# Re-laying a matrix product's input by DMA: 128-token blocks, repeated pooled rows and paired tokens in a fused attention and mixing kernel

## The chip, the cores and the metric

The kernel runs on one core of one Trainium2 chip. The time is the device time of that core, in microseconds (us). Every quoted time is a median of several executions, with the range behind it. Each execution is labelled fast or slow: with one core, a run is called slow when it is over 1.5% above the fastest run of the same kernel. The trace also gives the mean granted TensorE clock, as a share of full speed.

The engines are named as in the profile: PE (matmuls), PEld (weight loads, which overlap PE), DVE (VectorE), ACT (ScalarE), POOL (GpSimd) and SP (SyncE, which here does nothing but issue DMAs). "SPq" lines are DMA issues in SP's instruction stream. An issue is only the handing over of a transfer; the bytes move later, on 16 DMA engines.

## The reference, cut to what matters

There are 8 batches, 8 heads, 576 tokens and 64 numbers per head, so the model width is 512.

```python
def _attn_ref(q, k, v):                      # q, k, v: [8, 8, 576, 64]
    q_d, k_d, v_d = means over groups of 4 tokens        # 144 pooled tokens
    out_d = softmax_attention(q_d, k_d, v_d)
    out_up = np.repeat(out_d, 4, axis=2)                 # back to 576 tokens
    mask = np.abs(pos[:, None] - pos[None, :]) < 4
    out_local = masked softmax attention of q, k, v
    return out_up + out_local

def _moe_ref(x, w_theta, w_tok_r, w_tok_i, w_ch):        # x: [8, 576, 512]
    theta = x @ w_theta
    zr, zi = x * cos(theta), x * sin(theta)
    y = w_tok_r @ zr + w_tok_i @ zi                      # over the 576 tokens
    u = x + y
    return u + relu(u @ w_ch)
```

## The kernel before

The program emits three generators in an interleaved order: `attention(b+1)`, `modulate(b)` and `mix(b-1)`. One round of the three is called a batch period here. The names of the PSUM tiles name the steps:

- `attention`: `pstr` transposes q and k and pools them in the same matmul, `psvd` pools v, `psSd` and `psnd` are pooled scores and pooled output, `psS` and `psloc` are banded scores and local output, and `psup` repeats the pooled rows.
- `modulate`: `xTps` transposes x, and `psth` is theta.
- `mix`: `psu` is the token mix, `psr` and `psx` make the result.

The local attention works on five chunks of 120 tokens (the last has 96), and these chunks are kept through `modulate` and the token mix. So the token mix has 5 chunks x 2 (cosine and sine) = 10 steps of contraction, each with 120 of 128 rows in use.

```python
QS = [0, 120, 240, 360, 480]; QC = [120, 120, 120, 120, 96]      # query chunks
...
def load_qk(b):                                  # on SP, 256-byte rows
    for nm, src in (("q", q), ("k", k)):
        ...                                      # six DMAs each
        nc.sync.dma_start(out=t[:, c, :, :],
            in_=src[b, :, TR*c:TR*c+TR, :].rearrange("h p d -> p h d"))
...
    for h in range(H):                           # pooled output, K = 72 twice
        for kk in range(2):
            nc.tensor.matmul(out=pv[0:QD, h // 4, h % 4, :],       # psnd
                lhsT=pd[:, kk, h, QD*g:QD*g+QD], rhs=vd[:, kk, h, 0:65], ...)
...
    for c in range(NCH):                         # repeat pooled rows on PE, add on DVE
        nc.tensor.matmul(out=up[0:qn, :], lhsT=RT[g][:, QS[c]:QS[c]+qn],   # psup
                         rhs=xd[:, g, :], ...)
        ... psloc matmuls, rl = 1 / sum, tmp = psloc * rl ...
        nc.vector.tensor_tensor(out=x[0:cnt], in0=tmp[0:cnt], in1=up[0:cnt], op=ALU.add)
...
    # token mix: 4 x 5 x 2 x 2 = 80 matmuls per batch
    nc.tensor.matmul(out=pss[hf][:, 0:288],                        # psu
        lhsT=z[0:QC[c], c, ri, P*dc:P*dc+P],
        rhs=WT[0:QC[c], ri, c, 288*hf:288*hf+288], ...)
```

The softmax here doesn't subtract the row's maximum and nothing guards it: scores larger than these inputs give would overflow.

Of the kernel before, what the change touches and what calls it, by code (L numbers as in the profile page):

```python
# [13 lines left out]
P = 128  # L14
# [16 lines left out]
NCH = 5  # L31
TR = 96
NTR = S // TR
TP = TR // 4
TW = TR + TP

OS = [0, 128, 256, 384, 512]
OC = [128, 128, 128, 128, 64]
# [3 lines left out]
def kernel(  # L42
# [16 lines left out]
    xpool = ctx.enter_context(tc.tile_pool(name="xpool", bufs=1))  # L59
# [14 lines left out]
    def load_qk(b):  # L74
        ts = []
        for nm, src in (("q", q), ("k", k)):
            t = work.tile([TR, NTR, H, D], FP32, tag=f"{nm}32", bufs=1, name=f"{nm}32_{b}")
            for i in range(2):
                for c in range(3 * i, 3 * i + 3):
                    nc.sync.dma_start(  # L80
                        out=t[:, c, :, :],
                        in_=src[b, :, TR * c:TR * c + TR, :].rearrange("h p d -> p h d"),
                    )
            ts.append(t)
        staged[b] = ts

    def load_v(b):
        t = work.tile([P, NCH, H, D], FP32, tag="v32", bufs=1, name=f"v32_{b}")
        for c in range(NCH):
            nc.sync.dma_start(  # L90
                out=t[0:KW[c], c, :, :],
                in_=v[b, :, KS[c]:KS[c] + KW[c], :].rearrange("h p d -> p h d"),
            )
        staged[b].append(t)

    def cast(b, engines):

        q32, k32, v32 = staged.pop(b)
        q_tm = work.tile([TR, NTR, H, D], BF16, tag="q_tm", bufs=1, name=f"q_tm{b}")
        k_tm = work.tile([TR, NTR, H, D], BF16, tag="k_tm", bufs=1, name=f"k_tm{b}")  # L100
        v_w = work.tile([P, NCH, H, 66], BF16, tag="v_w", name=f"v_w{b}")
        inputs[b] = (q_tm, k_tm, v_w)
        nc.vector.memset(v_w[:, :, :, 64:65], 1.0)
        for eng, dst, src in ((engines[0], q_tm, q32), (engines[1], k_tm, k32)):
            for i in range(2):
                eng(out=dst[:, 3 * i:3 * i + 3], in_=src[:, 3 * i:3 * i + 3])  # L106
                yield
        engines[2](out=v_w[:, 0:2, :, 0:D], in_=v32[:, 0:2])
        yield
        engines[2](out=v_w[:, 2:4, :, 0:D], in_=v32[:, 2:4])  # L110
        engines[2](out=v_w[0:KW[4], 4, :, 0:D], in_=v32[0:KW[4], 4])
        yield

    load_qk(0)
    load_v(0)

# [5 lines left out]

    ip = const.tile([TR, TW], BF16, name="ip")
    nc.vector.memset(ip[:, TR:TW], 0.25)
    nc.gpsimd.affine_select(out=ip[:, TR:TW], in_=ip[:, TR:TW], compare_op=ALU.is_ge, fill=0.0,
                            base=0, pattern=[[-4, TP]], channel_multiplier=1)
    nc.gpsimd.affine_select(out=ip[:, TR:TW], in_=ip[:, TR:TW], compare_op=ALU.is_ge, fill=0.0,
                            base=3, pattern=[[4, TP]], channel_multiplier=-1)
    nc.vector.tensor_copy(out=ip[:, 0:TR], in_=ident[0:TR, 0:TR])  # L129

    pihc = const.tile([P, 1], FP32, name="pihc")
    nc.vector.memset(pihc, PIH)

    first = cast(0, (nc.vector.tensor_copy, nc.gpsimd.tensor_copy, nc.scalar.copy))
    for _ in range(4):
        next(first)
# [6 lines left out]
    for lo, hi, sh, w in ((0, 120, 0, QD), (4, 124, 59, 144)):  # L143
# [13 lines left out]
    def pool_mat(g, c):  # L157
        o = 0 if c == 0 else 59 - (KS[c] - 288 * g) // 4
        return PU[min(c, 1)][0:KW[c], o:o + QD]


    ru = const.tile([QD, 288 + S], BF16, name="ru")
    nc.vector.memset(ru, 1.0)
    nc.gpsimd.affine_select(out=ru, in_=ru, compare_op=ALU.is_ge, fill=0.0,
                            base=-288, pattern=[[1, 288 + S]], channel_multiplier=-4)
    nc.gpsimd.affine_select(out=ru, in_=ru, compare_op=ALU.is_ge, fill=0.0,
                            base=291, pattern=[[-1, 288 + S]], channel_multiplier=4)
    RT = [ru[:, 288 - 288 * g:288 - 288 * g + S] for g in range(2)]


    w_tm = []
    for ri, w_dram in enumerate((moe_w_tok_r, moe_w_tok_i)):
        t = moep.tile([P, 5, S], BF16, tag="uT", name=f"wtm{ri}")
        nc.gpsimd.dma_start(out=t[:, 0:4, :], in_=w_dram[0:512, :].rearrange("(c p) e -> p c e", p=P))
        nc.gpsimd.dma_start(out=t[0:64, 4, :], in_=w_dram[512:576, :])
        w_tm.append(t)
    wch = wpool.tile([P, 4, DM], BF16, name="wch")
    nc.gpsimd.dma_start(out=wch, in_=moe_w_ch.rearrange("(c p) e -> p c e", p=P))
    WT = wpool.tile([P, 2, NCH, S], BF16, name="WT")

    def build_WT():
        for ri in range(2):
            for c in range(NCH):
                ps = w1(f"wps{ri}{c}", BF16)
                for ct in range(5):
                    rows = OC[ct]
                    nc.tensor.transpose(  # L187
                        out=ps[0:QC[c], ct * P:ct * P + rows],
                        in_=w_tm[ri][0:rows, ct, QS[c]:QS[c] + QC[c]],
                        identity=ident[0:rows, 0:rows],  # L190
                    )
                nc.vector.tensor_copy(out=WT[0:QC[c], ri, c, :], in_=ps[0:QC[c], 0:S])
                yield
# [4 lines left out]
    def attention(b):  # L198
        q_tm, k_tm, v_w = inputs.pop(b)
        if b + 1 < B:  # L200
            load_qk(b + 1)
            load_v(b + 1)
        ahead = cast(b + 1, (nc.gpsimd.tensor_copy,) * 3) if b + 1 < B else iter(())
        qT = work.tile([P, 4, S], BF16, tag="qT", name=f"qT{b}")
        kT = work.tile([P, 4, S], BF16, tag="kT", name=f"kT{b}")
        qdT = work.tile([P, 4, SD], BF16, tag="qdT", name=f"qdT{b}")
        kdT = work.tile([P, 4, SD], BF16, tag="kdT", name=f"kdT{b}")
        for n, (tm, To, Tdo) in enumerate(((q_tm, qT, qdT), (k_tm, kT, kdT))):
            for hh in range(4):
                ps = w2(f"pstr{n}{hh}_{b}")  # L210
                for c in range(NTR):
                    nc.tensor.matmul(  # L212
                        out=ps[:, c // 3, (c % 3) * TW:(c % 3) * TW + TW],
                        lhsT=tm[:, c, 2 * hh:2 * hh + 2, :],
                        rhs=ip,
                        start=True, stop=True,
                    )
                pv = ps[:, :, 0:3 * TW].rearrange("p k (c w) -> p k c w", w=TW)
                nc.scalar.copy(  # L219
                    out=To[:, hh, :].rearrange("p (k c w) -> p k c w", k=2, c=3),  # L220
                    in_=pv[:, :, :, 0:TR],
                )
                nc.vector.tensor_copy(
                    out=Tdo[:, hh, :].rearrange("p (k c w) -> p k c w", k=2, c=3),
                    in_=pv[:, :, :, TR:TW],
                )
                yield

        vd = work.tile([QD, 2, H, 66], BF16, tag="vd", name=f"vd{b}")
        nc.vector.memset(vd[:, :, :, 64:65], 1.0)  # L230
        for g, cs in ((0, (0, 1, 2)), (1, (2, 3, 4))):
            ps = w1(f"psvd{g}_{b}")
            for c in cs:
                nc.tensor.matmul(
                    out=ps[0:QD, :],
# [4 lines left out]
            nc.scalar.copy(out=vd[:, g, :, 0:D], in_=ps[0:QD, :].rearrange("p (h d) -> p h d", d=D))  # L240
# [3 lines left out]
        pd = work.tile([QD, 2, H, SD], BF16, tag="pd", name=f"pd{b}")  # L244

        def pooled_scores(dst, kk, hh):
            for par in range(2):
                nc.tensor.matmul(
                    out=dst(par),
                    lhsT=kdT[64 * par:64 * par + 64, hh, QD * kk:QD * kk + QD],  # L250
# [4 lines left out]
        for kk in range(2):  # L255
            ps = w2(f"psSd{kk}_{b}")
            for hh in range(3):
                pooled_scores(lambda par: ps[0:QD, par, SD * hh:SD * hh + SD], kk, hh)
            nc.scalar.activation(  # L259
                out=pd[:, kk, 0:6, :].rearrange("p (j e) w -> p e j w", e=2),  # L260
                in_=ps[0:QD, :, 0:3 * SD].rearrange("p e (j w) -> p e j w", w=SD),
                func=AF.Exp, scale=SCL,
            )
            yield
        ps = w2(f"psSd2_{b}")
        for kk in range(2):
            pooled_scores(lambda par: ps[0:QD, par, SD * kk:SD * kk + SD], kk, 3)
        nc.scalar.activation(
            out=pd[:, :, 6:8, :].rearrange("p k e w -> p e k w"),
            in_=ps[0:QD, :, 0:2 * SD].rearrange("p e (k w) -> p e k w", w=SD),  # L270
            func=AF.Exp, scale=SCL,
        )
        yield
# [3 lines left out]
        for c in range(NCH):  # L277
            kw, qn = KW[c], QN[c]
            ps = w2(f"psS{c}_{b}")
            for hh in range(4):  # L280
                for par in range(2):
# [6 lines left out]
            pm = work.tile([P, 8, P], BF16, tag="pm", bufs=6, name=f"pm{c}_{b}")  # L288
            nc.scalar.activation(  # L289
                out=pm[0:kw, :, 0:qn],  # L290
# [3 lines left out]
            off = KS[c] - QS[c] + 3  # L294
            nc.gpsimd.affine_select(out=pm[0:kw, :, 0:qn], in_=pm[0:kw, :, 0:qn],  # L295
                                    compare_op=ALU.is_ge, fill=0.0,
                                    base=off, pattern=[[0, 8], [-1, qn]], channel_multiplier=1)
            nc.gpsimd.affine_select(out=pm[0:kw, :, 0:qn], in_=pm[0:kw, :, 0:qn],  # L298
                                    compare_op=ALU.is_ge, fill=0.0,
# [156 lines left out]
    def drain(gen):  # L456
        for _ in gen:
            pass
# [55 lines left out]
```

## Time and profile before

| what | before |
|---|---|
| time | 359.72 us, median of 3 (359.23 to 360.01); 359.87 with a fourth run, which the ratio below counts |
| span in the trace, granted clock | 358.8 us, 0.955 |
| first `psth` (end of the prologue) | 63.4 us |
| distances between the first `psth` of successive batches | 33.4, 38.2, 37.7, 37.8, 36.1, 36.1, 35.4 us |
| last first-`psth` to the end | 40.7 us |

These lines are from the page of the kernel before: busy time by engine, and the span in 40 slices of 9 us (a digit is the busy share of a slice in tenths; the last row is what the DMA engines moved).

```profile
PE 296.6 (83%) x2834; PEld 201.8 (56%) x2834; DVE 193.5 (54%) x435; ACT 192.1 (54%) x283; POOL 156.2 (44%) x153
...
PE   0025689948799989999899989998999899979995
...
GB/s 151 200 187 198 181 154 156 193 178 14 48 200 27 5 180 173 195 53 175 179 195 79 117 218 174 118 145 153 0 3 62 74 0 3 81 53 2 117 16 132
```

PE is the busiest engine and, after the prologue, stays near 9 tenths. The first six slices are low on PE while the DMA row is at its highest: the prologue is fed by DMA.

These are two windows of 4 us from the windows view of one period of the kernel before. The columns are the window, its length, then busy us and instruction count of PE, PEld, DVE, ACT and POOL, then the clock, the DMA share and the GB/s.

```profile
203.00:207.00 4.00, 3.81 (x39) 2.12 (x36) 4.00 (x9) 0.71 (x2) 1.70 (x2) 1.00 0.62 171
...
219.00:223.00 4.00, 4.00 (x36) 2.90 (x33) 2.09 (x6) 2.23 (x4) 1.95 (x2) 1.00 1.33 209
```

In the first (the `psr`/`psloc` half of a period) DVE is busy for all of its 4.00 us; in the second (the `psu`/`psth` half) PE is. A period therefore has a DVE-bound half and a PE-bound half.

This is the timeline of SP in one period of the kernel before: start, us, engine, line, operation, transfer, count.

```profile
217.45 4.92 SPq L80 DMA_DIRECT2D q<-in_q_dram  x6
226.85 3.00 SPq L80 DMA_DIRECT2D k<-in_k_dram  x5
236.27 0.37 SPq L452 DMA_DIRECT2D out_dram<-osb  x1
...
238.32 1.16 SPq L90 DMA_DIRECT2D v<-in_v_dram  x2
...
245.69 0.47 SPq L452 DMA_DIRECT2D out_dram<-osb  x1
```

SP has long gaps, most of them waits for the next output to be ready. The 22 issues of a period (six each for q and k, five each for v and the output) leave it idle for more than half of the time.

### The profile page before, as it was taken

What the parts mean: (1) busy time and instruction counts of PE and PEld (TensorE: products, weight loads), DVE (VectorE), ACT (ScalarE), POOL (GpSimd) and SP (SyncE); (2) the same over time, 40 slices, a digit from 0 to 9 for tenths busy, and PEclk for the clock granted to TensorE, in tenths of its full rate; (3) what the DMA queues carried; (4) which work ended last, traced back from release to release, by engine and by line L of the source; (5) the groups of instructions that cost most, each with busy time, mean ns of one, the idle gap of its engine ahead of it and who ended that gap; (6) DMA issues with size and microseconds to landing.
All of it is one profiled execution on the core that took longest, in us unless ns stands there. A gap on an engine that the chain in (4) does not pass through costs nothing.

```text
span 358.8 us, 7037 instructions
## 1 busy us (share of the span) xinstructions
PE 296.6 (83%) x2834; PEld 201.8 (56%) x2834; DVE 193.5 (54%) x435; ACT 192.1 (54%) x283; POOL 156.2 (44%) x153
## 2 busy tenths in 40 slices
PE   0025689948799989999899989998999899979995
PEld 0023368526566656665666666656665676657672
DVE  1121076533754494629574876287628752865433
ACT  1024802585267735782669366936693679334303
POOL 8011396308831783377147817583458003700000
PEclk9999999985589998999899999999999999999999
DMA  8999989990291069936994499766001200210303
GB/s 151 200 187 198 181 154 156 193 178 14 48 200 27 5 180 173 195 53 175 179 195 79 117 218 174 118 145 153 0 3 62 74 0 3 81 53 2 117 16 132
DMA packets 122577, 41.18 MB, mean 115 GB/s; under 512 B 115760, under 2 KB 117936, under 8 KB 122544
## 3 DMA queue, kind: packets, MB, share of 16 engines
q1 hardware_dynamic: 120272, 38.35, 55.2%
q0 software_dynamic: 2272, 2.38, 4.0%
q8 instruction: 22, 0.36, 0.4%
q14 instruction: 11, 0.09, 0.1%
HBM read 33.65 MB, written 9.44 MB: 120 GB/s over the span
## 4 chain that ended last, share of the span: by engine, by line
PE 47%; DVE 20%; ACT 15%; SPq 7%; issue 4%; POOL 3%; DMA 3%; POOLq 0%; ACTq 0%
PE psu L421 18%; PE psth L396 9%; SPq L80 6%; PE psr L439 6%; DVE osb L451 4%; DVE tmp L355 4%; DVE z L405 4%; DVE x L362 4%; PE pstr L212 3%; ACT pd L259 3%; PE psS L282 3%; ACT L259 2%; PE psnd L311 2%; PE wps L187 2%; ACT vd L240 2%
## 5 line engine op out<-in xcount | busy, mean ns | idle before, releaser
L421 PE MATMUL psu<-WT,z 120*128 120x288 bf16 (+1 forms) x640 | 93.6, 292 | 2.5 <-DVE uT L430 2.5
L421 PEld LDWEIGHTS <-z 120*128 120x128 bf16 (+1 forms) x640 | 60.5, 100 | 23.2 <-issue 3.6
L295 POOL TENSOR_SCALAR_AFFINE_SELECT pm<-pm 128x1024 bf16<-128x1024 bf16 (+1 forms) x40 | 41.2, 1047 | 65.5 <-ACT pm L289 65.5
L449 ACT ACTIVATE rel<-psr 128x512 f32<-128x512 f32 (+1 forms) x40 | 23.8, 596 | 61.7 <-PE psr L439 61.7
L430 DVE TENSOR_TENSOR uT<-psu,xT 128x288 bf16<-128x288 f32 x64 | 26.8, 452 | 50.7 <-PE psu L421 50.7
L396 PE MATMUL psth<-wth,xT 128*120 128x512 bf16 (+1 forms) x160 | 45.1, 406 | 7.6 <-DVE xT L386 6.8
L405 DVE TENSOR_TENSOR z<-cs,x 120x1024 bf16<-120x1024 bf16 (+1 forms) x40 | 39.1, 977 | 17.4 <-ACT cs L404 17.3
L219 ACT CAST qT<-pstr 128x576 bf16<-128x576 f32 x32 | 20.3, 640 | 52.1 <-PE pstr L212 52.1
L403 ACT ACTIVATE cs<-psth,pihc 120x512 bf16<-120x512 f32 (+1 forms) x40 | 27.5, 687 | 35.8 <-PE psth L396 35.6
L106 POOL CAST k_tm<-k 96x1536 bf16<-96x1536 f32 x16 | 24.5, 1547 | 41.6 <-DMA k<-in_k_dram 17.5
L439 PE MATMUL psr<-wch,uT 128*128 128x512 bf16 (+1 forms) x160 | 42.1, 379 | 0.0
L298 POOL TENSOR_SCALAR_AFFINE_SELECT pm<-pm 128x1024 bf16<-128x1024 bf16 (+1 forms) x40 | 41.1, 1047 | 0.3
L106 POOL CAST q_tm<-q 96x1536 bf16<-96x1536 f32 x14 | 23.2, 1679 | 40.5 <-PE pstr L212 32.2
L212 PE MATMUL pstr<-ip,q_tm 96*128 96x120 bf16 x192 | 19.8, 249 | 21.8 <-DVE ip L129 11.8
L289 ACT ACTIVATE pm<-psS 128x1024 bf16<-128x1024 f32 (+1 forms) x40 | 36.4, 981 | 1.9 <-PE psS L282 1.5
L451 DVE TENSOR_TENSOR osb<-rel,psx 128x512 f32<-128x512 f32 (+1 forms) x40 | 27.3, 682 | 7.9 <-ACT rel L449 7.1
L396 PEld LDWEIGHTS <-xT 128*120 128x120 bf16 (+1 forms) x160 | 20.5, 139 | 17.3 <-DVE xT L386 8.1
L212 PEld LDWEIGHTS <-q_tm 96*128 96x128 bf16 x192 | 14.6, 115 | 26.5 <-DVE ip L129 11.8
L386 DVE COPY xT<-xTps 128x480 bf16<-128x480 bf16 (+1 forms) x40 | 15.5, 389 | 25.7 <-PE xTps L381 25.6
L355 DVE TENSOR_TENSOR tmp<-psloc,rl 120x512 bf16<-120x512 f32 (+1 forms) x40 | 26.9, 685 | 0.1
L362 DVE TENSOR_TENSOR x<-tmp,psup 120x512 bf16<-120x512 bf16 (+1 forms) x40 | 26.5, 675 | 0.0
L346 PEld LDWEIGHTS <-pm 128*128 128x128 bf16 (+1 forms) x320 | 17.2, 113 | 15.9 <-issue 7.3
(68 smaller groups left out, 417.6 us busy)
## 6 DMA issues: line engine op xcount, KB each, us to landing
q<-in_q_dram SPq DMA_DIRECT2D x48, 192.0 KB, 5.6
k<-in_k_dram SPq DMA_DIRECT2D x48, 192.0 KB, 4.9
v<-in_v_dram SPq DMA_DIRECT2D x32, 256.0 KB, 5.3
out_dram<-osb SPq DMA_DIRECT2D x32, 256.0 KB, 2.0
v<-in_v_dram SPq DMA_DIRECT2D x8, 200.0 KB
out_dram<-osb SPq DMA_DIRECT2D x8, 128.0 KB
wtm<-in_moe_w_tok_r_dram POOLq DMA_DIRECT2D x1, 576.0 KB, 9.3
wtm<-in_moe_w_tok_i_dram POOLq DMA_DIRECT2D x1, 576.0 KB, 12.0
```

The source lines that it names most:

```text
L106: eng(out=dst[:, 3 * i:3 * i + 3], in_=src[:, 3 * i:3 * i + 3])
L212: nc.tensor.matmul(out=ps[:, c // 3, (c % 3) * TW:(c % 3) * TW + TW], lhsT=tm[:, c, 2 * hh:2 * hh + 2, :], rhs=ip, start=True, stop=True,)
L289: nc.scalar.activation(out=pm[0:kw, :, 0:qn], in_=ps[0:kw].rearrange("p e (j w) -> p (e j) w", w=P)[:, :, 0:qn], func=AF.Exp, scale=SCL,)
L295: nc.gpsimd.affine_select(out=pm[0:kw, :, 0:qn], in_=pm[0:kw, :, 0:qn], compare_op=ALU.is_ge, fill=0.0, base=off, pattern=[[0, 8], [-1, qn ...
L298: nc.gpsimd.affine_select(out=pm[0:kw, :, 0:qn], in_=pm[0:kw, :, 0:qn], compare_op=ALU.is_ge, fill=0.0, base=6 - off, pattern=[[0, 8], [1, ...
L355: nc.vector.tensor_tensor(out=tmp[0:cnt].rearrange("p (j e d) -> p e j d", e=2, j=4), in0=pv[0:cnt, :, :, 0:D], in1=rl[0:cnt].unsqueeze(3) ...
L362: nc.vector.tensor_tensor(out=x[0:cnt], in0=tmp[0:cnt], in1=up[0:cnt], op=ALU.add)
L396: nc.tensor.matmul(out=th[0:cnt, :], lhsT=xT[:, dc, QS[c]:QS[c] + cnt], rhs=wth[:, dc, :], start=(dc == 0), stop=(dc == 3),)
L405: nc.vector.tensor_tensor(out=z[0:cnt, c, :, :], in0=cs[0:cnt], in1=xt[c][0:cnt].unsqueeze(1).to_broadcast([cnt, 2, DM]), op=ALU.mult,)
L421: nc.tensor.matmul(out=pss[hf][:, 0:288], lhsT=z[0:QC[c], c, ri, P * dc:P * dc + P], rhs=WT[0:QC[c], ri, c, 288 * hf:288 * hf + 288], star ...
L439: nc.tensor.matmul(out=psr[0:cnt, :], lhsT=uT[:, dc, OS[c]:OS[c] + cnt], rhs=wch[:, dc, :], start=(dc == 0), stop=(dc == 3),)
L451: nc.vector.tensor_tensor(out=osb[0:cnt], in0=rel[0:cnt], in1=psx[0:cnt, 0:DM], op=ALU.add)
```

## The change

The intent is to relieve both halves. Token-mix chunks of a full 128 tokens need nine steps of contraction instead of ten (four blocks of cosine, four of sine, and one that holds the last 64 tokens of both). For this x must stand in 128-token blocks, while the local attention gives 120-token chunks, so DMAs copy the pieces from SBUF to SBUF. The repetition of the pooled rows moves from PE to DMA as well, and the five adds on DVE, which read PSUM, become two larger bf16 adds from SBUF. q and k are loaded as pairs of tokens, so a row has 512 bytes instead of 256, in three DMAs each instead of six. The last block of the result is computed as two column halves on 128 partitions. The emission order is new, the selects of the first batches become DVE multiplies, and the weights are loaded later and transposed during the first period.

```diff
-QD = 72                                  # pooled keys per group, twice
+KG = [(0, 90), (90, 54)]                 # pooled keys: groups of 90 and 54
+QG = [(0, 96), (96, 48)]                 # pooled queries: groups of 96 and 48
@@ load
-    in_=src[b, :, TR*c:TR*c+TR, :].rearrange("h p d -> p h d")            # 6 each
+    in_=src[b, :, TB*c:TB*c+TB, :].rearrange("h (p r) d -> p h (r d)", r=2)  # 3 each
@@ attention: the transposed copy puts the token pairs back in order
-    out=To[:, hh, :].rearrange("p (k c w) -> p k c w", k=2, c=3), in_=pv[:, :, :, 0:TR]
+    out=To[:, hh, :].rearrange("p (c w r) -> p c r w", c=NTR, r=2), in_=<psum, r then w>
@@ attention: pooled output, loops as before (for h: for kk:)
-    lhsT=pd[:, kk, h, QD*g:QD*g+QD],     rhs=vd[:, kk, h, 0:65]
+    lhsT=pd[0:rows, kk, h, q0:q0+m],     rhs=vd[0:rows, kk, h, 0:65]      # rows = 90, 54
@@ attention: repeat the pooled rows
-    psup matmuls on PE
+    for blk in ((0, 1, 2) if g == 0 else (3, 4)):
+        for t0 in ((0, 64) if blk == 4 else (0,)):
+            for r in range(4):
+                nc.sync.dma_start(out=xrep[t0+r:t0+BW[blk]:4, blk, :], in_=xd[p0:p0+n, g, :])
@@ attention: re-lay the local output
-    nc.vector.tensor_tensor(out=x[0:cnt], in0=tmp[0:cnt], in1=up[0:cnt], op=ALU.add)
+    for p1 in ...:                                                  # 10 pieces a batch
+        nc.sync.dma_start(out=t128[p1:p1+n, blk, :], in_=tmp[...])
@@ modulate
+    add(0, 2); transposes(0); add(2, 5)    # x = t128 + xrep, two adds on DVE
@@ mix: 72 matmuls a batch
-    lhsT=z[0:QC[c], c, ri, ...], rhs=WT[0:QC[c], ri, c, ...]        # 5 chunks x 2
+    lhsT=z[:, i, ...],           rhs=WT[:, i, ...]                  # 9 chunks
@@ (cut: column halves of the last block, masks by DVE in the first batches,
@@  weight transposes inside the first period, new emission order)
```

In the profile of the changed kernel the tile t128 appears as `t`.

## The prediction

> **What bounds the kernel now.** The page: span 358.8 us, PE busy 83%, DVE and ACT 54%. The windows view gives three stages.
> (1) Prologue, 0 to 62.5 us: DMA is saturated (180 to 215 GB/s). The last k cast ends at 30 us, v lands near 36. The timeline shows POOL's affine selects back to back from 41.5 to 53 and weight transposes from 54 to 62.5.
> (2) Seven batch periods: 33.5, 39, 37.7, 37.9, 36.0, 36.1, 35.3 us.
> (3) Tail 40.8 us, PE at its pace.
> A 36 us period has two halves. First 23 us (psu, psth, pstr): PE work paced back to back sums to about 21.4, so PE-bound, ACT close behind. Last 13 us (psr, psloc, psup): PE needs about 9.7, but DVE is 4.00 of 4.00 us busy in several windows: per chunk osb 0.68, rl 0.2, tmp 0.68, x 0.67, plus xd; DVE-bound. Then PE waits 1.0 us at the boundary for xT, behind that backlog.
>
> **What changes, per batch.**
> PE: psu 80 to 72 matmuls at 0.1225 us (40 took 4.91): -1.0. psup gone, six at 0.216: -1.3. psvd 6 to 5: -0.2. pstr 120 to 144 columns: +0.5. Full-width transposes +0.1. Sum -1.9.
> DVE: five x adds (3.4 us, a PSUM input) leave the DVE-bound half; two bf16 SBUF adds (estimate 0.7 + 0.95, from z's unblocked 0.68 for 1024) go to the first half. Half-width osb -0.3, smaller z -0.3 or more.
> ACT: one sine less, 0.6; half of a relu, 0.2.
> DMA: q and k packets of 512 instead of 256 bytes. The Trainium skill, "DMA: Bandwidth & Descriptors", Specifications, gives 512 B as the least for line rate; no run yet shows it. Added: 24 + 10 small SBUF copies on SP, 1.3 MB, roughly 2 us to land (output DMAs: 2.0), covered by a psu half and two pstr steps before modulate.
>
> **Critical share.** Steady first half 23 to about 22.2. Second half 13 to about 10.5: without the adds and the psup matmuls, DVE and PE both need about 7.5 to 8, and POOL's selects (10.3 us after the first score exp) become the next limit. Period about 33.1, so -3. I expect 33 us for each of b=2 to 6 and 35 for b=1: -22 in all.
> Prologue: cheaper q/k loads (estimate: v lands near 28 rather than 36), band masks as DVE multiplies (about 0.7 us) instead of 2.1 us POOL pairs, transposes overlapped: first modulate near 44.5 instead of 62.5: -18. First period, partly on DVE masks: about -5.
> Tail: 16 psu fewer, half-width last block: -2.4.
> Sum -47: **312 us**, 80% range **300 to 327**. Faster by over 2%: 0.97; same 0.02; slower 0.01.
>
> **What would show it.** First psth near 45 us; steady periods 32 to 34; DVE below 90% in the psr windows and no psth wait on xT behind tmp; psloc waiting on POOL pm; each q/k load taking about 60% of its old time; no long waits on t128 or xrep.
>
> **What would make it wrong.** The in-order SP queue: 34 more issues per batch may delay loads or outputs. Weight DMAs still issued first and taking the bandwidth. DVE SBUF adds and multiplies blocked by POOL: the Trainium skill, "SBUF — State Buffer", says the two share a port pair held for a whole instruction; this trace agrees (z 0.68 alone, 1.5 to 1.77 beside POOL casts). POOL casts falling between the selects: periods of 35. ACT (22 of the first 23 us) hiding the PE saving.

## More of the kernel before

The group of the pooled output, and one 16-matmul piece of it in PE's timeline, both of the kernel before, are needed later as well. A group's columns are line, engine, operation, out<-in, shape and count, then busy us and mean ns of one, then the idle time before it.

```profile
L311 PE MATMUL psnd<-vd,pd 72*72 72x65 bf16 x256 | 12.8, 211 | 0.7 <-ACT pm L289 0.7
```

```profile
233.52 0.71 PE L311 MATMUL psnd<-vd,pd 72*72 72x65 bf16 x16
```

The shape "72*72 72x65" says that 72 rows are contracted (K = 72). Sixteen such matmuls take 0.71 us.

## The result, and the profile after

The changed kernel is correct and takes 413.97 us, median of 4 runs (412.6 to 415.58). The ratio to the kernel before is 1.151, with a 95% interval of 1.146 to 1.156. Here and below a ratio is the mean time of one kernel's fast runs over that of the other's of the same rounds, so it is not quite the ratio of the quoted medians. The prediction was 312 us.

The corresponding lines of the page after:

```profile
PE 332.0 (81%) x2741; PEld 213.8 (52%) x2741; DVE 194.1 (47%) x415; ACT 196.2 (48%) x272; POOL 146.2 (36%) x157
...
PE   0478732897799979998899879997999679937995
...
GB/s 181 208 209 218 140 41 88 204 153 39 85 205 153 39 157 185 190 57 116 152 205 106 46 161 224 155 42 159 182 194 56 115 77 2 50 119 78 0 116 115
```

PE has fewer instructions and more busy time, at a lower granted clock (0.874 against 0.955). In the DMA row, slices near 200 GB/s alternate with slices near 40 GB/s. A batch period is now 43.2 to 44.8 us (the last 40.3), and the first `psth` starts at 68.2 us.

This is SP's timeline over one whole period of the kernel after, the counterpart of the one above:

```profile
201.08 1.72 SPq L87 DMA_DIRECT2D q<-in_q_dram  x3
202.90 5.74 SPq L87 DMA_DIRECT2D k<-in_k_dram  x3
208.74 9.00 SPq L95 DMA_DIRECT2D v<-in_v_dram  x5
217.84 17.26 SPq L387 DMA_DIRECT2D xrep<-xd  x24
235.20 1.01 SPq L543 DMA_DIRECT2D out_dram<-osb  x2
236.31 2.34 SPq L432 DMA_DIRECT2D t<-tmp  x3
238.70 0.58 SPq L543 DMA_DIRECT2D out_dram<-osb  x1
239.38 2.96 SPq L432 DMA_DIRECT2D t<-tmp  x4
242.44 0.52 SPq L543 DMA_DIRECT2D out_dram<-osb  x1
243.01 1.82 SPq L432 DMA_DIRECT2D t<-tmp  x3
244.94 1.18 SPq L546 DMA_DIRECT2D out_dram<-osb  x2
246.21 1.15 SPq L87 DMA_DIRECT2D q<-in_q_dram  x2
```

There is no gap longer than 0.12 us. From one q load (201.08) to the next (246.21) SP issues for 45.1 us, which is as long as a batch period. Of this, the 24 copies of `xrep` take 17.3 us and the 10 copies of `t` 7.1 us, so 24.4 us are new. These copies are small: `xrep` moves 16 or 32 KB at a time and `t` 8 to 120 KB. Yet each occupies the queue for about 0.7 us.

The view of one source line gives the duration of one issue (minimum, median and maximum in ns):

```profile
L387 SPq DMA_DIRECT2D xrep<-xd x192: 482/592/1513, 45.5 to 364.1; - x192
```

```profile
L432 SPq DMA_DIRECT2D t<-tmp x80: 530/594/1597, 62.0 to 374.8; - x80
```

The medians are 592 and 594 ns; some 0.1 us lies between issues. Nor does an issue follow the bytes or the rows of its copy: read one by one from the trace, the medians of the `t` copies are 0.71 us for 8 KB, 0.54 for 16 KB, 0.57 for 112 KB and 0.90 for 120 KB. These two, one after the other in SP's timeline, hand over 8 rows (8 KB) and 112 rows (112 KB):

```profile
237.31 0.72 SPq L432 DMA_DIRECT2D t<-tmp  x1
238.08 0.57 SPq L432 DMA_DIRECT2D t<-tmp  x1
```

While `xrep` is issued, the DMA engines are not what is short. In the windows view of the kernel after, these are the stretch of the v load and the one in which SP issues the second half of `xrep`:

```profile
209.00:217.80 8.80, 8.80 (x67) 5.90 (x65) 3.94 (x6) 2.94 (x5) 4.93 (x5) 1.00 1.05 192
...
227.00:235.20 8.20, 7.09 (x87) 5.50 (x84) 5.61 (x14) 4.18 (x7) 3.75 (x5) 1.00 0.15 36
```

During the v load the engines move 192 GB/s; during that part of `xrep` they move 36 GB/s, with a busy share of 0.15. The loads are another matter: their issues take 16.5 us of the 45.1, and those of v about 1.8 us each in a stretch with a busy share of 1.05 (0.6 us each in the timeline before). That part of SP's time goes with full DMA engines; the 24.4 us of copies do not.

What this does to the rest is in the waits and the timeline of the kernel after. First the largest waits of PE and of DVE on this path (total us, times, longest), then the prologue and its end in time order:

```profile
PE xTps L454 <- DVE t L449: 26.5, 6, 10.9
```

```profile
DVE t L449 <- DMA t<-tmp: 27.9, 10, 8.4
```

```profile
44.78 0.69 DVE L421 TENSOR_TENSOR tmp<-psloc,rl 96x512 bf16<-96x512 f32 x1
...
45.53 16.38 SPq L387 DMA_DIRECT2D xrep<-xd  x24
...
62.02 7.49 SPq L432 DMA_DIRECT2D t<-tmp  x10
...
66.35 0.69 DVE L449 TENSOR_TENSOR t<-t,xrep 128x1024 bf16<-128x1024 bf16 x1 [8.41 <-DMA t<-tmp]
...
67.10 1.03 PE L454 MATMUL xTps<-ident,t 128*128 128x128 bf16 x8 [10.95 <-DVE t L449]
...
68.23 1.89 PE L466 MATMUL psth<-wth,xT 128*128 128x512 bf16 x4
```

The compute of the first attention is done at 45.5 us, 1 us later than predicted for the first modulate. But only then does SP reach the first `xrep` issue, because the next batch's loads stand before it in the queue (the first `xd` was ready at 34.6 us), and 24 us of issues follow. The first `psth` comes at 68.2 us rather than at 45.

A second, unpredicted difference is in the pooled output. Its group and one piece of it in the timeline, both of the kernel after:

```profile
L368 PE MATMUL psnd<-vd,pd 54*96 54x65 bf16 (+3 forms) x256 | 43.0, 234 | 0.0
```

```profile
212.28 2.58 PE L368 MATMUL psnd<-vd,pd 90*96 90x65 bf16 x16
```

The same number of matmuls of the same width takes 43.0 us in all instead of 12.8, and a piece of 16 takes 2.58 us instead of 0.71. The mean ns of one hardly moves (211 to 234), because that is the length of an instruction, and what grew is the distance between their starts. The two contracted halves now have 90 and 54 rows and alternate within the inner loop.

So there are two theories. **A, the queue:** the period is the sum of the issue times on SP. **B, PE:** the alternating `psnd` and the lower clock make PE slower, and SP merely follows. Under B the wait on `t` would shrink as PE got faster. A third, **C**, is that the copies' bytes or their landing time matter, not their number.

### The profile page after: what moved, and what is told of

Its sections match the earlier page's. It is cut to its first block, busy times and chain, and to the rows that moved or that the text cites. A ratio compares the mean times of both kernels' runs of the same rounds, so it can differ in the third digit from the quotient of the medians.

```text
span 411.4 us, 7155 instructions
## 1 busy us (share of the span) xinstructions
PE 332.0 (81%) x2741; PEld 213.8 (52%) x2741; DVE 194.1 (47%) x415; ACT 196.2 (48%) x272; POOL 146.2 (36%) x157
## 4 chain that ended last, share of the span: by engine, by line
PE 56%; SPq 11%; ACT 9%; DVE 8%; POOL 6%; DMA 5%; issue 3%; DVEq 0%; ACTq 0%
PE psu L494 18%; PE psnd L368 9%; PE psth L466 9%; SPq L387 7%; PE pstr L252 4%; PE psr L514 4%; ACT kT L260 3%; DMA k<-in_k_dram 3%; SPq L432 3%; PE psS L329 3%; PE psvd L277 3%; POOL pm L352 2%; PE xTps L454 2%; DMA t<-tmp 2%; POOL pm L350 2%
## 5 line engine op out<-in xcount | busy, mean ns | idle before, releaser
L494 PE MATMUL psu<-WT,z 128*128 128x288 bf16 x576 | 88.9, 306 | 0.0
L494 PEld LDWEIGHTS <-z 128*128 128x128 bf16 x576 | 56.9, 104 | 23.4 <-issue 6.5
L466 PE MATMUL psth<-wth,xT 128*128 128x512 bf16 x160 | 48.7, 436 | 3.7 <-DVE xT L455 2.3
L474 ACT ACTIVATE cs<-psth,pihc 128x512 bf16<-128x512 f32 x32 | 22.0, 687 | 56.9 <-PE psth L466 55.6
L124 POOL CAST q_tm<-q 96x1024 bf16<-96x1024 f32 x21 | 24.4, 1164 | 57.3 <-DMA q<-in_q_dram 51.4
L368 PE MATMUL psnd<-vd,pd 54*96 54x65 bf16 (+3 forms) x256 | 43.0, 234 | 0.0
L454 PE MATMUL xTps<-ident,t 128*128 128x128 bf16 x160 | 18.0, 260 | 26.5 <-DVE t L449 26.5
L514 PE MATMUL psr<-wch,uT 128*128 128x512 bf16 x128 | 38.8, 404 | 0.0
L539 ACT ACTIVATE rel<-psr 128x512 f32<-128x512 f32 (+1 forms) x40 | 22.3, 556 | 34.6 <-PE psr L514 25.8
L368 PEld LDWEIGHTS <-pd 54*96 54x96 bf16 (+3 forms) x256 | 29.3, 115 | 14.4 <-issue 1.0
L124 POOL CAST k_tm<-k 96x1024 bf16<-96x1024 f32 x24 | 25.5, 1062 | 29.3 <-DMA k<-in_k_dram 27.8
L449 DVE TENSOR_TENSOR t<-t,xrep 128x1024 bf16<-128x1024 bf16 (+1 forms) x16 | 16.3, 1018 | 28.0 <-DMA t<-tmp 27.9
L476 DVE TENSOR_TENSOR z<-cs,t 128x1024 bf16<-128x1024 bf16 x32 | 26.5, 836 | 5.0 <-ACT cs L475 4.9
```

Of the source, the lines that this page charges most:

```text
L124: eng(out=dst[:, c].rearrange("p r h d -> p h r d"), in_=src[:, c].rearrange("p h (r d) -> p h r d", r=2))
L368: nc.tensor.matmul(out=pv[0:m, h // 4, h % 4, :], lhsT=pd[0:rows, kk, h, q0:q0 + m], rhs=vd[0:rows, kk, h, 0:65], start=(h % 4 == 0 and kk ...
L454: nc.tensor.transpose(out=ps[:, dc, :], in_=x[:, c, P * dc:P * dc + P], identity=ident)
L466: nc.tensor.matmul(out=th, lhsT=xT[:, dc, P * c:P * c + P], rhs=wth[:, dc, :], start=(dc == 0), stop=(dc == 3),)
L494: nc.tensor.matmul(out=pss[hf][:, 0:288], lhsT=z[:, i, P * dc:P * dc + P], rhs=WT[:, i, 288 * hf:288 * hf + 288], start=(i == 0), stop=(i ...
L514: nc.tensor.matmul(out=psr, lhsT=uT[:, dc, P * c:P * c + P], rhs=wch[:, dc, :], start=(dc == 0), stop=(dc == 3),)
```

## The experiments

Twelve kernels ran. They ran in three sets: 1 to 4; then 5, 6, 7 and 10; then 8, 9, 11 and 12. All give the right result, except one that is marked. In each set the kernel before ran on the same chip, with medians of 359.58, 359.62 and 357.8 us. Its seven runs in a set spread over 5 to 6 us, from about 354.6 us up. Most gains here are larger than that, but differences of under 1% between two experiments should be read with care.

### 1. The kernel after, with the two loops of `psnd` exchanged

```diff
-            for h in range(H):
-                for kk in range(2):
+            for kk in range(2):
+                for h in range(H):
```

All eight matmuls with 90 rows now come first, then the eight with 54. Nothing changes on the other engines.

> The changed kernel with the loops over key group and head in the pooled output (psnd) exchanged, so that K=90 and K=54 matmuls no longer alternate; the order of the SP, ACT and POOL programs is unchanged. Theory A (the SP queue's issue time, about 44 us per batch, is the period): psnd x16 falls from 2.4-2.8 us to about 0.7-1.0 us, but the time stays within 2% of the changed kernel's 414 us (405 to 418) and the periods stay near 44 us. Rival B (PE is the limit, through the slow psnd and a lower clock): about 7 x 3.9 us come off, 380 to 390 us.

Measured: 410.86 us (406.98 to 411.38), ratio 1.145 (1.134 to 1.157), clock 0.883. The piece of 16 is nearly as fast as before the change (timeline of this experiment):

```profile
207.36 0.98 PE L368 MATMUL psnd<-vd,pd 90*96 90x65 bf16 x16
```

The whole group, and PE's wait on `t`, in this experiment:

```profile
L368 PE MATMUL psnd<-vd,pd 90*96 90x65 bf16 (+3 forms) x256 | 15.3, 208 | 0.5 <-ACT pm L337 0.5
```

```profile
PE xTps L454 <- DVE t L449: 37.8, 10, 15.3
```

The group fell from 43.0 to 15.3 us busy, yet the periods stayed at 42.0 to 45.7 us (the last 39.0). PE work that was 28 us shorter gained some 3 us. PE's wait on `t` did not shrink, as B would have it, but grew from 26.5 to 37.8 us: a faster PE only waits longer. As long as SP is full, B's part matters little: that is A.

### 2. The kernel after, with `xrep` issued from POOL

```diff
-                        nc.sync.dma_start(out=xrep[...], in_=xd[...])
+                        nc.gpsimd.dma_start(out=xrep[...], in_=xd[...])
```

> The changed kernel with its 24 xrep copies per batch issued from the POOL queue instead of SP; same copies, same bytes[...]. Theory A (SP issue time): SP needs about 28 us per batch, the periods fall from 44 to 36-40 us, total 350 to 380 us. Rival B (PE) and rival C (the DMA engines, or the latency of a copy chain through SBUF): no gain, 405 us or more. A POOL that waits in order for xd may give some of the gain back.

Measured: 430.67 us (425.13 to 433.56), ratio 1.192 (1.175 to 1.210). This missed the expectation, in direction too: as it was written, 405 us or more spoke for B or C. The profiled run is a slow one (clock 0.814), so its absolute times are not compared; only who waits for whom, and the length of an issue, are read from it. First the group of the issues, then the waits of PE and of SP:

```profile
L387 POOL DMA_DIRECT2D xrep<-xd x192 | 98.2, 516 | 24.8 <-DVE xd L376 18.2 <-DMA xrep<-xd 4.5 <-issue 2.0
```

```profile
PE psloc L412 <- POOL pm L352: 38.9, 19, 5.6
```

```profile
SPq L543 <- DVE osb L541: 148.1, 25, 31.3
```

SP is free now: it waits 148 us for outputs. But the issue costs about the same on POOL, 516 ns each and 98.2 us in all, and POOL has the selects of the band mask (`pm`) in the same in-order stream. PE's `psloc` now waits 38.9 us for these selects. The work was moved, not removed. So an issue costs about as much on the other queue; but this run alone does not decide between A and its rivals. Experiments 1, 3 and 5 do.

### 3 and 4. The pooled rows repeated by matmul again, without and with the exchanged loops

```diff
-            (the 24 xrep DMAs)
+    # in modulate, for each of the five 128-token blocks
+    up = w1(f"psup{c}_{b}")
+    nc.tensor.matmul(out=up, lhsT=ru[0:m, t:t + P], rhs=xd[0:m, g, :], start=True, stop=True)
+    nc.vector.tensor_tensor(out=x[:, c, :], in0=x[:, c, :], in1=up, op=ALU.add)
```

Everything else of the change stays, the 10 copies to 128-token blocks too. The second of the pair also has the loops of experiment 1.

> The changed kernel with the xrep copies undone: the pooled rows are repeated by a matmul into PSUM, in the 128-token blocks, and DVE adds block by block from PSUM (PE +1.3 us, DVE about +1.8 us per batch, SP -16.6 us). Theory A: periods 36-39 us, 345 to 370 us. Rival B (PE): no gain or slower, 410 to 425 us. Rival C also expects a gain, so this run alone does not separate A from C.

> xrep undone and the psnd loops exchanged. Theory A: with SP no longer the limit the psnd fix now pays, periods 33-35 us, total 318 to 338 us, so 3.9 us per batch more than xrep_mm saves. If psnd does not pay here either (within 2% of xrep_mm), PE is not the limit after SP and something else (ACT, or the wait for the t128 copies) is.

Measured: without the exchanged loops 387.71 us (380.86 to 388.94); only one of its runs counts as fast, so there is no ratio. With them 344.79 us (344.18 to 346.46), ratio 0.965 (0.955 to 0.975). Both are slower than expected; the first missed by 18 us (11 by its one fast run), the second by 7. Undoing the 24 issues alone takes off 26 us by the medians (33 us by the one fast run). After that, exchanging the loops is worth a further 43 us by the medians (36 by the fast runs), where it was worth some 3 us in experiment 1. So both causes are real, and they are not additive: the second hides behind the first. Once SP has slack, B's part pays.

The group of `psnd` is 44.2 us busy in the first and 15.2 us in the second, and their granted clocks are 0.887 and 0.956. The extra 29 us on PE explain most of the difference. Here, and between the kernel before and experiment 10, the lower clock goes with the slow `psnd`. But experiment 1 has a fast `psnd` and a clock of 0.883, so `psnd` is not all of it; what causes the lower clock was not tested.

### 5. The kernel after, with twice as many `xrep` issues for the same bytes

```diff
-                        nc.sync.dma_start(out=xrep[..., blk, :], in_=xd[p0:p0+n, g, :])
+                        for cc in range(2):
+                            nc.sync.dma_start(out=xrep[..., blk, 256*cc:256*cc+256],
+                                              in_=xd[p0:p0+n, g, 256*cc:256*cc+256])
```

> The changed kernel with each of the 24 xrep copies per batch cut into two of half the columns: the same bytes, twice the issues. Theory A (SP issue time, about 0.69 us each whatever the size): 24 more issues are about 14 to 17 us more per batch, periods near 59-61 us, total 510 to 550 us. Rival C (bytes on the DMA engines or latency to land): within a few per cent of 414 us, at most 435.

Measured: 538.25 us (two runs, 536.43 and 540.07), ratio 1.503 (1.480 to 1.526), inside the expected range. One line of SP's timeline of this experiment shows why:

```profile
278.61 33.01 SPq L388 DMA_DIRECT2D xrep<-xd  x48
```

Twice the issues of half the size take 33.0 us instead of 17.3, which is 15.7 us more, and the periods grew from about 44 us to between 57 and 61 us. The bytes are the same, so C falls as far as it rests on bytes, and a longer landing would not lengthen SP's own issue time. Cutting the columns also doubles the number of row pieces, but the copies of 8 and 112 rows above show no cost per row. The time is per issue. This is the sharpest test of A.

### 6. Experiment 4 with a contiguous write of the transposed q and k

In the changed kernel ACT writes the transposed q and k with a stride of two elements, to put the token pairs in order. Here the strided side is the read from PSUM.

```diff
-                    out=To[:, hh, :].rearrange("p (c w r) -> p c r w", c=NTR, r=2),
-                    ... ap=[..., [TR + TP, 2], [1, TR]]
+                    out=To[:, hh, :].rearrange("p (c w r) -> p c w r", c=NTR, r=2),
+                    ... ap=[..., [1, TR], [TR + TP, 2]]
```

> xrep_mm_psnd with ACT's copy of the transposed q and k reading PSUM interleaved and writing contiguously, instead of writing every other element; only the order inside ACT's program changes. If the write with stride 2 is what made a copy 0.80 us instead of 0.64: back to about 0.65 us, ACT -1.2 us per batch, and as ACT is nearly full in the first part of a period, 334 to 340 us. If ACT is not what limits: 343 to 347 us. If the read with stride costs the same: copies stay at 0.80.

Measured: 342.49 us (340.77 to 344.49), ratio 0.957 (0.947 to 0.966). The copies are cured, as these groups of experiment 4 (with the exchanged loops) and of this experiment show:

```profile
L267 ACT CAST qT<-pstr 128x576 bf16<-128x576 f32 x32 | 25.4, 803 | 46.0 <-PE pstr L259 45.7
```

```profile
L267 ACT CAST qT<-pstr 128x576 bf16<-128x576 f32 x32 | 20.3, 638 | 48.5 <-PE pstr L259 48.4
```

The mean falls from 803 to 638 ns (it was 640 in the kernel before and 800 in the kernel after), some 10 us of ACT time for q and k together, but the time falls by 2 us only. The expectation of 334 to 340 missed: these copies were not the limit.

### 7, 8 and 9. Taking issues off SP, and moving the turn of `modulate`

Three kernels start from experiment 6. In 7 the ten `t` copies are issued from ACT, in 8 the outputs are, and 9 is 8 with a new first line of the emission order, in which `modulate` takes its first turn later.

```diff
 7
-                    nc.sync.dma_start(out=t128[p1:p1 + n, blk, :], in_=tmp[...])
+                    nc.scalar.dma_start(out=t128[p1:p1 + n, blk, :], in_=tmp[...])
 8
-                nc.sync.dma_start(out=out[b, P * c:P * c + P, :], in_=osb)
+                nc.scalar.dma_start(out=out[b, P * c:P * c + P, :], in_=osb)
 9, on top of 8
-        "x a a m x a m a x m a x m a a m a m "
+        "x a a x a m a m a x m a x m a m a m "
```

> mm_contig with the ten t128 copies per batch issued from ACT's queue instead of SP. They no longer stand behind the loads of the next batch in the prologue (first psth 5 to 8 us earlier) nor behind outputs. ACT issues about 6 us per batch more, in the part of the period where it has slack: 325 to 338 us. If the issue time lands where ACT is full, or ACT waits in order for tmp: no gain or slower than mm_contig.

> mm_contig with the six output DMAs per batch issued from ACT's queue, so that SP issues only the t128 copies at the end of a period. In mm_contig SP issues outputs and t128 copies without a gap for 12 us there, the last t128 lands late, PE stands 2.0 us before the transposes and the next psu x10 runs at half clock (2.5 instead of 1.5 us). If that SP backlog is why the periods are 36 and not 33 us: the wait on t128 falls below 1 us, periods 33.5 to 34.5, total 326 to 335 us. If not: 339 to 345 us.

> mm_contig_oact with the first modulate step of a period one psu half and one pstr step later in the program, so that more PE work covers the landing of the last t128 copy. If a wait on t128 is left: 2 to 8 us faster than mm_contig_oact. If none is left: equal, or up to 6 us slower, because the sines then crowd against the exps on ACT.

Measured: 7 takes 339.08 us (336.15 to 342.2), ratio 0.944 (0.928 to 0.959), just outside its range. 8 takes 337.82 us (333.29 to 340.59), ratio 0.936 (0.926 to 0.945), outside too by its median; its two fast runs, 336.86 and 333.29 us, lie around the upper end of the range. 9 takes **333.31 us** (332.26 to 334.56), ratio 0.931 (0.925 to 0.936). It beats both kernels, and its gain over 6 is clear, since the two intervals do not meet. Over 8 it gains 4.5 us by the medians, but two of 8's four runs are slow: by the fast runs it gains 1.7 us, and the intervals overlap. So the expected 2 to 8 us of this last step are not shown.

The reason for 9 was read from the period boundary of experiment 6 (its timeline, DVE and PE):

```profile
229.44 0.69 DVE L459 TENSOR_TENSOR t<-t,psup 128x512 bf16<-128x512 bf16 x1 [1.86 <-DMA t<-tmp]
...
230.18 0.38 PE L464 MATMUL xTps<-ident,t 128*128 128x128 bf16 x4 [2.01 <-DVE t L459]
```

Here PE sits idle for 2.0 us, in its own order, for copies that SP issued only from 226.25 us on, behind two outputs and other copies. In 9 the copies have more time, and the total waits show it. DVE's wait on `t` is 13.2 us in experiment 6, 10.0 in 8 (whose profiled run is a slow one) and 3.6 in 9; PE's is 5.7, 3.4 and 1.8 us. These are PE's in 6 and in 9:

```profile
PE xTps L464 <- DVE t L459: 5.7, 5, 2.0
```

```profile
PE xTps L464 <- DVE t L459: 1.8, 2, 1.0
```

The seven periods of 9 are 33.8, 38.3, 35.9, 34.3, 34.0, 33.4 and 31.9 us (before: 33.4, 38.2, 37.7, 37.8, 36.1, 36.1, 35.4). So the gain that the prediction expected of the steady state, a period of 33 us, is nearly there from the fourth period on, once the queue, the loop order and the turn are mended.

### 10 and 11. The kernel before, with unequal contraction in `psnd`

The kernel before contracts 72 rows twice. Two controls shorten the second half, to 64 rows and to 68.

```diff
-                        lhsT=pd[:, kk, h, QD * g:QD * g + QD],
-                        rhs=vd[:, kk, h, 0:65],
+                        lhsT=pd[0:QD - 8 * kk, kk, h, QD * g:QD * g + QD],     # 11: QD - 4 * kk
+                        rhs=vd[0:QD - 8 * kk, kk, h, 0:65],
```

Both leave out pooled keys. The first has a relative error of 0.026, too large for a right result.

> The kernel before with one thing changed: psnd's second key group uses 64 of its 72 rows, so K alternates 72, 64, 72, 64. The result is wrong on purpose (8 of 144 pooled keys are dropped in the product and the sum); the order on every engine is unchanged. If alternating K across 64 rows is what makes psnd slow: psnd x16 goes from 0.71 us to 2.0-2.8 us, total 370 to 388 us. If the slowness in the changed kernel comes from its other sizes (90 and 54 rows, 96 and 48 columns): no change, 357 to 362 us.

> The control to the run with K alternating 72 and 64: here 72 and 68 rows, wrong on purpose in the same way. If any change of K from one matmul to the next costs: psnd x16 over 2 us again and about 400 us. If only crossing 64 rows costs[...]: psnd x16 stays at 0.71 us and the time at 355 to 362 us.

Measured: with 72 and 64 rows 401.2 us (396.53 to 403.93), ratio 1.116 (1.101 to 1.131); the direction was right, the size larger than expected. With 72 and 68 rows 360.6 us (two runs), ratio 1.007 (0.998 to 1.015). The groups of the two (the first from a run in the slow state):

```profile
L311 PE MATMUL psnd<-vd,pd 72*72 72x65 bf16 (+1 forms) x256 | 46.5, 248 | 0.7 <-ACT pm L289 0.7
```

```profile
L311 PE MATMUL psnd<-vd,pd 72*72 72x65 bf16 (+1 forms) x256 | 12.8, 210 | 0.7 <-ACT pm L289 0.7
```

Alternating between unequal numbers of rows costs nothing as such. Alternating between 72 and 64 costs 34 us of PE time over 256 matmuls, 0.13 us each, in a kernel where nothing else was changed (the traces of the changed kernel and of experiment 1, both fast, give 28 us, 0.11 us each, for 90 and 54 rows). The Trainium skill, "TensorEngine Tiling (Array Packing)", section Key Properties, says that changing the tiling mode drains TensorE, and its section Performance Considerations counts a contraction of 64 or fewer rows as a case for 2x row tiling. The step between 68 and 64 rows agrees with that. But the trace has no field for the mode, so the drain is the likely reason and not a shown one.

### 12. The kernel before, with the token pairs alone

Only the loads of q and k as pairs were brought over, with the contiguous copy of experiment 6.

> The kernel before with one part of the change alone: q and k loaded as token pairs (512-byte rows, three DMAs of 384 KB each instead of six of 192 KB), cast and transposed from there, with the contiguous copy by ACT. If the pairs shorten the prologue: first psth 4 to 8 us earlier than 63.4 us, periods unchanged at 35-38 us, total 350 to 357 us. If 512-byte rows bring nothing: 359 to 364 us (pstr has 24 more columns).

Measured: 344.65 us (342.65 to 346.59), ratio 0.962 (0.954 to 0.970), better than expected. Its DMA row on the page is:

```profile
GB/s 169 257 216 217 239 259 188 140 225 61 122 163 138 94 170 162 139 64 171 175 123 94 131 164 138 105 105 1 2 13 111 17 0 3 124 16 2 131 9 138
```

The first slices reach 257 and 259 GB/s, where the kernel before had 218 at most in any slice. The Trainium skill, "DMA: Bandwidth & Descriptors", section Specifications, gives 512 bytes as the least size for line rate, and this run agrees in direction. It halves the number of these DMAs as well, from six to three, and no run separates the two. The first `psth` starts at 53.6 us instead of 63.4, and from the third on all periods are 35.8 us. So this smallest part of the change brings about 13 us by itself (fast runs of its set), more than half of what the best version gains (24 to 25 us).

## Why the prediction was wrong, point by point

1. **The step that failed.** It is "Added: 24 + 10 small SBUF copies on SP, 1.3 MB, roughly 2 us to land (...), covered by a psu half and two pstr steps before modulate". The step costed the landing of a copy, and the cover that one copy would have. That cost was about right: in experiment 2 an `xrep` copy landed 2.5 us after its issue from POOL in the median. It did not cost the issue. Measured, an issue takes 0.59 us plus about 0.1 us to the next, the 34 take 24.4 us per batch, and SP is in order. With the 17 other issues, which take 19.8 us here, that makes a period of 45 us. The term was listed as a risk ("The in-order SP queue"), but without a number, and the number was to be had: in the trace before, the median SP issue takes 0.36 us for an output and 0.82 us for a q load. With these an estimate for 34 issues is 12 to 28 us; added to the 14 us of issues in SP's timeline before, it comes to 26 to 42 us, beside a period of 33 us that was hoped for.
2. **A missing term.** `psnd` was taken as unchanged. Alternating K between 90 and 54 costs 28 us of PE time (43.0 against 15.3 us). In the changed kernel it hides behind SP (about 3 us); without the SP limit it is worth 36 to 43 us, part of which goes with a lower clock.
3. **A sign that failed: "no long waits on t128 or xrep".** DVE waits 27.9 us for the `t` copies, and PE 26.5 us behind it.
4. **The prologue.** "First modulate near 44.5" was right for the compute (45.5 us) and wrong for the data (68.2 us). In the best version it is 53.2 us: the loads are faster, but the copies and the matmul repeat still lie behind the first attention.
5. **The weights.** The fear that weight DMAs would be issued first came true only for those of theta, at 1.3 us as before; the others, issued at 6.0 to 8.8 us before, are issued at 19.7 to 24.5 us now. What they cost was not tested.
6. **What was right.** The adds left the DVE-bound half: in windows of 4 us, DVE's fullest in a period of the kernel after has 3.65 of 4.00 us, where before it had 4.00. The longer period thins DVE's work out too, so this is weak evidence. (In experiment 9 the adds read PSUM again, and two windows are nearly full, but no long wait of PE follows from it.) The smaller token mix shows in its instruction count, 576 against 640. The steady period of 33 us was nearly reached (33.4 to 34.3 us) by experiment 9, which still repeats rows on PE. Paired loads help, as expected, and gained more by themselves than expected (344.65 us where 350 to 357 were expected).

Where the predicted 47 us stand in experiment 9: the prologue gives 10.2 us of the 18 expected (63.4 to 53.2 us), the seven periods 13.0 us of the 27 expected (254.7 to 241.7 us), and the tail 4.4 us where 2.4 were expected (40.7 to 36.3 us). The second and third periods still take 38.3 and 35.9 us. What holds these back was not examined by an experiment. In the trace of 9, PE still waits 3.9 us for the selects on POOL, and ACT is 56% busy, so there is no single next limit.

## What to carry to other kernels

Before replacing an engine's work by many small copies, multiply their number by the time of one issue in the queue that will carry them, and lay the sum beside that queue's timeline: here an in-order queue with no gap left set the period, although the copies' bytes were few. Before moving issues to another engine, look for slack in that engine's own order: on POOL they made the kernel slower (experiment 2). When a change makes two neighbouring matmuls differ in the number of contracted rows, compare the time of the piece of 16 in the timeline before and after, and group equal shapes together.

## What the Trainium skill lacked or had wrong

- "DMA: Bandwidth & Descriptors", section "Issuing engines are not separate DMA queues", says that issuing from several engines only saves the sequencer's time to start a DMA, "which is usually small relative to the DMA itself". Here it was not small: 0.59 us median for a copy of 8 to 120 KB on SP, 24.4 us of a 45 us period, with the DMA engines at a busy share of 0.15 in the second half of `xrep`. The page's rule to coalesce transfers under 64 KB agrees with experiment 5. But the page gives about 0.6 us only as a first-byte latency (Specifications). A time for which the issuing queue is taken stands there only as a count of sequencer cycles for earlier generations, in its part on trn3 B0, and no rule says to multiply it by the number of copies. "Perfetto Trace Analysis", section "Optimizing DMA Performance", does name the case, a sequencer track that is solid with DMA slices, and the timeline after agrees with it.
- The same page, section "Anatomy of one DMA — SWDGE (gpsimd) path", puts the dispatch of a DMA from POOL at about 50 ns and calls the making of its descriptors small. Here each of 192 issues took POOL 516 ns in the mean (experiment 2; spans on POOL are rough), and the selects behind them in its order came late: `psloc` waited 38.9 us for them.
- "TensorEngine Tiling (Array Packing)", Key Properties, says that changing the mode drains TensorE, but gives no cost, and does not say that a plain matmul of 64 or fewer rows can meet it. Here alternating 72 and 64 rows cost 0.13 us per matmul (experiment 10), and 72 and 68 nothing (experiment 11).
- "ScalarE: Activation LUTs" gives one element per cycle for every function, with no word on strides (the skill's page on SBUF treats them, which was not compared here). A 128x576 copy from PSUM took 800 ns with a write stride of two bf16 elements and 638 ns with a contiguous write and a strided read (experiment 6).
